# Banded attention in 48-query blocks, values stationary, pipelined by batch with the MLP

A kernel that ran attention over all keys and then an MLP is replaced by one that computes only a band, and runs the MLP of one batch inside the attention of the next. The question is what that does to the time, and what sets the time of the new kernel.

## The chip, the cores and the metric

One core of one Trainium2 chip. Times are device microseconds (us) of one execution. A core has engines that run side by side: PE (TensorE matmuls; PEld is its weight load), DVE (VectorE), ACT (ScalarE), POOL (GpSimd), SP (SyncE, which here only starts transfers). PE writes its results into tiles in PSUM (`psA` and the `ps_` pools below); another engine reads a tile there, and until it has, PE waits with the next result for that tile.

## The reference, cut to what matters

Shapes: 8 batches, 8 heads, 576 positions, head size 64; then 4608 tokens of width 512, and a hidden width of 2048. The result is float32.

```python
scores = scale * np.matmul(q, k.transpose(0, 1, 3, 2))
mask = np.abs(pos[:, None] - pos[None, :]) <= 32
mask = mask | is_global[:, None] | is_global[None, :]     # 8 global positions
scores = np.where(mask, scores, -1000000000.0)
attn = softmax(scores)                                    # cut: max, exp, sum
x = (attn @ v), heads side by side, 4608 x 512
h = x @ w_in
s = np.sin(alpha * h)
g = h + s * s / (alpha + 1e-09)
return g @ w_out
```

A query outside the global set therefore needs 65 keys around it and the 8 global keys. Only the 8 global queries need all 576 keys.

## The kernel before: what the change touches

It works on one pair of heads after the other. For each head it computes all 576 x 576 scores, multiplies the exponentials by a 0/1 mask, and multiplies with the values, where the exponentials are the stationary operand. The values carry a column of ones, so that the softmax sum comes out beside them. Only when all 8 batches are done does the MLP start. All weights are scaled on DVE, and they are first used at 470 us. (`...` marks cuts.)

```python
for b in range(B):
    ...
    for hp in range(NHP):                       # 4 pairs of heads
        ...                                     # transposes of q and k
        for t in range(2):
            for g in range(NKG):
                for gi in range(GK):            # 6 key tiles of 96 in all
                    nc.tensor.matmul(out=scm[:, gi, :], lhsT=kTh[:, k0 : k0 + KW], rhs=qTh[:, 0:SM], ...)
                    nc.tensor.matmul(out=sct[:, gi, :], lhsT=kTh[:, k0 : k0 + KW], rhs=qTh[:, SM:S], ...)
                nc.scalar.activation(out=E[...], in_=scm[:, :, :], func=AF.Exp, scale=scale)
                nc.scalar.activation(out=E[...], in_=sct[:, :, :], func=AF.Exp, scale=scale)
                nc.vector.tensor_tensor(out=E[...], in0=E[...], in1=MASK[...], op=ALU.mult)
            for qb in range(NQB):
                for kt in range(NKT):
                    nc.tensor.matmul(out=avq[0:qrows, qb, :], lhsT=E[:, kt, qs0 : qs0 + qrows],
                                     rhs=VS[:, hh * NKT + kt, :], ...)
            ...                                 # reciprocal and normalization on DVE, transposes to xT
for tci in range(NCHUNK):                       # the MLP, 9 chunks of 512 tokens
    for nt in range(NT):
        for c in range(CT):
            nc.tensor.matmul(out=h2[:, :tn], lhsT=w_inp[:, c, nt * P : (nt + 1) * P],
                             rhs=xT[:, c, t0 : t0 + tn], ...)
        nc.scalar.activation(out=Sb[:, :tn], in_=h2[:, :tn], func=AF.Sin)
        nc.vector.tensor_tensor(out=S2[:, :tn], in0=Sb[:, :tn], in1=Sb[:, :tn], op=ALU.mult)
        nc.vector.tensor_tensor(out=H2b[:, nt, :tn], in0=h2[:, :tn], in1=S2[:, :tn], op=ALU.add)
    ...                                         # second matmul, copy, store
```

The softmax here doesn't subtract the row's maximum and nothing guards it: scores larger than these inputs give would overflow.

## Time and profile before

| kernel before | value |
|---|---|
| median of 3 runs | 733.84 us (732.45 to 734.54) |
| profiled span | 732.5 us |
| PE busy | 642.0 us, 88% |
| DVE, ACT, POOL busy | 56%, 47%, 15% |
| granted PE clock | 1.00 throughout |

The head of the page gives the busy time of each engine and its share of the span; the PE row cuts the span into 40 slices, a digit being the busy share in tenths.

```profile
PE 642.0 (88%) x4360; PEld 352.6 (48%) x4384; DVE 412.0 (56%) x893; ACT 341.7 (47%) x566; POOL 107.7 (15%) x144
...
PE   0000699999999999999999999999999999999997
```

The PE row has a quiet start of four slices, one slice at six tenths, and is at nine tenths or more from there almost to the end. Where PE is full, PE is what to save. The windows view says it in numbers; the columns are the stretch, its length, then busy time (with the number of instructions) of PE, PEld, DVE, ACT and POOL, the granted clock, the DMA share and GB/s.

```profile
0.00:79.00 79.00, 0.64 (x6) 0.61 (x7) 37.67 (x62) 0.00 (x0) 40.31 (x60) 1.00 1.51 165
250.00:350.00 100.00, 100.00 (x842) 62.14 (x841) 58.44 (x143) 58.92 (x99) 22.47 (x28) 1.00 0.90 37
```

PE is busy in 100.00 of 100.00 us in the middle of the attention. In the first 79 us it does nothing worth naming. The waits view gives for each wait the engine and its line, the engine that released it, then the total, the number of times and the longest.

```profile
PE psx L237 <- POOL identb masks.py:199: 43.0, 1, 43.0
PE psx L237 <- DVE qT L242: 36.0, 2, 35.5
```

The chain of waits (the page's fourth part) is the work that ended last, followed back. It is PE's:

```profile
PE 83%; issue 6%; DVE 3%; POOL 3%; DMA 2%; ACT 2%; DVEq 0%; ACTq 0%; POOLq 0%
```

In the groups (line, engine, operation, output<-inputs, shape, count, then total busy us and mean ns, then idle time before it) the score and value matmuls are the attention's largest cost:

```profile
L259 PE MATMUL scm<-qT,kT 64*96 64x512 bf16 x384 | 202.2, 646 | 2.0 <-ACT E L273 0.9
L297 PE MATMUL avq<-VS,E 96*128 96x65 bf16 (+1 forms) x1920 | 143.3, 245 | 1.1 <-DVE E L285 0.8
```

### The profile page before, as it was taken

The page shows a single profiled execution, that of the slowest core. Times are in us where ns is not written, and L with a number is a line of the kernel's source. Part 1 is how long each engine was busy: PE and PEld are TensorE (multiplying, and loading weights), DVE is VectorE, ACT ScalarE, POOL GpSimd, SP SyncE. Part 2 cuts the span into 40 slices and gives each one's busy share as a digit, 9 for nine tenths or more (in the row PEclk, how much of TensorE's full clock was granted, in tenths as well). Part 3 has the DMA queues.
Part 4 walks back from the last instruction along what each step waited for, and adds up shares of the span by engine and source line. Part 5 has one row for each costly group of instructions (what it writes and reads, how often), then busy time and mean ns, then how long its engine had stood idle before and what let it go on. Part 6 is the DMA issues. An engine that isn't in the chain of part 4 may idle for free.

```text
span 732.5 us, 10762 instructions
## 1 busy us (share of the span) xinstructions
PE 642.0 (88%) x4360; PEld 352.6 (48%) x4384; DVE 412.0 (56%) x893; ACT 341.7 (47%) x566; POOL 107.7 (15%) x144
## 2 busy tenths in 40 slices
PE   0000699999999999999999999999999999999997
PEld 0000356555665656565656666544444444444443
DVE  2466355555565655555555565594483573673762
ACT  0000465655565655555555565553353353353442
POOL 5167040122140131221500000000000000000000
PEclk9999999999999999999999999999999999999999
DMA  9999264918993999559968000001101001001001
GB/s 244 294 46 122 5 41 27 34 12 55 33 61 21 23 62 33 33 34 34 66 19 15 1 1 1 1 1 57 44 16 58 30 29 57 30 30 57 29 31 57
DMA packets 122529, 33.74 MB, mean 46 GB/s; under 512 B 115184, under 2 KB 115184, under 8 KB 121840
## 3 DMA queue, kind: packets, MB, share of 16 engines
q0 software_dynamic: 112256, 14.16, 49.3%
q1 hardware_dynamic: 10224, 18.89, 7.2%
q8 instruction: 34, 0.56, 0.3%
q14 instruction: 15, 0.12, 0.1%
HBM read 37.77 MB, written 9.44 MB: 64 GB/s over the span
## 4 chain that ended last, share of the span: by engine, by line
PE 83%; issue 6%; DVE 3%; POOL 3%; DMA 2%; ACT 2%; DVEq 0%; ACTq 0%; POOLq 0%
PE scm L259 21%; PE avq L297 17%; PE ops L383 17%; PE psx L237 5%; PE sct L266 5%; PE xps L329 2%; DMA QS<-in_q_dram 2%; DVE H2b L374 1%; ACT E L273 1%; POOL VS L79 1%; ACT Sb L369 1%; PE xps L335 1%; DVE Cq L111 1%; POOL KS L72 0%; POOL QS L72 0%
## 5 line engine op out<-in xcount | busy, mean ns | idle before, releaser
L273 ACT ACTIVATE E<-scm 96x1024 bf16<-96x1024 f32 x192 | 195.8, 1020 | 41.1 <-PE scm L259 35.8
L259 PE MATMUL scm<-qT,kT 64*96 64x512 bf16 x384 | 202.2, 646 | 2.0 <-ACT E L273 0.9
L285 DVE TENSOR_TENSOR E<-E,MASK 96x1152 bf16<-96x1152 bf16 x192 | 143.2, 747 | 24.9 <-ACT E L279 24.7
L297 PE MATMUL avq<-VS,E 96*128 96x65 bf16 (+1 forms) x1920 | 143.3, 245 | 1.1 <-DVE E L285 0.8
L297 PEld LDWEIGHTS <-E 96*128 96x128 bf16 (+1 forms) x1920 | 116.5, 135 | 53.1 <-issue 16.1
L383 PE MATMUL ops<-w_outp,H2b 128*128 128x512 bf16 x565 | 139.1, 379 | 0.6
L279 ACT ACTIVATE E<-sct 96x128 bf16<-96x128 f32 x192 | 51.8, 270 | 114.8 <-PE sct L266 114.4
L361 PEld LDWEIGHTS <-w_inp 128*128 128x128 bf16 x576 | 56.1, 98 | 74.3 <-issue 10.5
L383 PEld LDWEIGHTS <-H2b 128*128 128x128 bf16 x576 | 55.5, 98 | 68.8 <-DVE H2b L374 5.1
L266 PEld LDWEIGHTS <-kT 64*96 64x96 bf16 x384 | 58.4, 181 | 35.7 <-issue 26.7
L266 PE MATMUL sct<-qT,kT 64*96 64x64 bf16 x384 | 66.8, 264 | 0.0
L259 PEld LDWEIGHTS <-kT 64*96 64x96 bf16 x384 | 58.1, 173 | 15.3 <-issue 3.0
L391 ACT COPY osb<-ops 128x512 f32<-128x512 f32 x36 | 21.1, 585 | 84.3 <-PE ops L383 84.3
L237 PE MATMUL psx<-identb,QS 96*128 96x96 bf16 x192 | 21.9, 277 | 43.0 <-POOL identb masks.py:199 43.0
L237 PE MATMUL psx<-identb,KS 96*128 96x96 bf16 x192 | 26.2, 276 | 36.0 <-DVE qT L242 36.0
L305 DVE RECIPROCAL rec<-avq 128x4 f32<-128x4 f32 x64 | 11.7, 183 | 78.6 <-PE avq L297 78.6
L72 POOL DMA_DIRECT2D QS<-in_q_dram x48 | 36.9, 777 | 79.3 <-PE psx L237 78.5
L237 PEld LDWEIGHTS <-QS 96*128 96x128 bf16 x192 | 14.7, 133 | 57.2 <-issue 48.7
L237 PEld LDWEIGHTS <-KS 96*128 96x128 bf16 x192 | 15.4, 130 | 50.6 <-issue 50.6
L72 POOL DMA_DIRECT2D KS<-in_k_dram x48 | 36.9, 775 | 17.2 <-PE psx L237 15.1
L273 ACT ACT_TABLE_LOAD x1 | 1.3, 1283 | 81.5 <-PE sct L266 81.5
L242 DVE COPY kT<-psx 128x576 bf16<-128x576 bf16 x32 | 14.6, 455 | 33.0 <-PE psx L237 33.0
(614 smaller groups left out, 592.7 us busy)
## 6 DMA issues: line engine op xcount, KB each, us to landing
out_dram<-osb SPq DMA_DIRECT2D x36, 256.0 KB, 2.0
QS<-in_q_dram POOLq DMA_DIRECT2D x48, 96.0 KB, 3.6
KS<-in_k_dram POOLq DMA_DIRECT2D x48, 96.0 KB, 3.8
VS<-in_v_dram POOLq DMA_DIRECT2D x8, 576.0 KB, 11.1
wtmp<-in_moe_w_in_dram SPq DMA_DIRECT2D x4, 1024.0 KB, 8.4
alphaB<-in_moe_alpha_dram SPq DMA_DIRECT2D x1, 1024.0 KB, 5.8
wtmp_4073<-in_moe_w_out_dram SPq DMA_DIRECT2D x1, 1024.0 KB, 12.2
wtmp_4079<-in_moe_w_out_dram SPq DMA_DIRECT2D x1, 1024.0 KB, 10.4
```

The source lines that it names most:

```text
L72: nc.gpsimd.dma_start(out=dstS[:, jt, :, :], in_=src[b, :, jt * KW : (jt + 1) * KW, :].rearrange("h p d -> p h d"),)
L237: nc.tensor.transpose(out=psx[:, jt * KW : (jt + 1) * KW], in_=srcS[:, jt, 2 * hp : 2 * hp + 2, :], identity=identb[0:KW, 0:KW],)
L259: nc.tensor.matmul(out=scm[:, gi, :], lhsT=kTh[:, k0 : k0 + KW], rhs=qTh[:, 0:SM], start=True, stop=True,)
L266: nc.tensor.matmul(out=sct[:, gi, :], lhsT=kTh[:, k0 : k0 + KW], rhs=qTh[:, SM:S], start=True, stop=True,)
L273: nc.scalar.activation(out=E[:, g * GK : (g + 1) * GK, 0:SM], in_=scm[:, :, :], func=AF.Exp, scale=scale,)
L279: nc.scalar.activation(out=E[:, g * GK : (g + 1) * GK, SM:S], in_=sct[:, :, :], func=AF.Exp, scale=scale,)
L285: nc.vector.tensor_tensor(out=E[:, g * GK : (g + 1) * GK, :], in0=E[:, g * GK : (g + 1) * GK, :], in1=MASK[0:KW, g * GK : (g + 1) * GK, :] ...
L297: nc.tensor.matmul(out=avq[0:qrows, qb, :], lhsT=E[:, kt, qs0 : qs0 + qrows], rhs=VS[:, hh * NKT + kt, :], start=(kt == 0), stop=(kt == NK ...
L329: nc.tensor.transpose(out=xps[:, qs0 : qs0 + QB], in_=xnp[:, qb, :], identity=identb[:, :],)
L361: nc.tensor.matmul(out=h2[:, :tn], lhsT=w_inp[:, c, nt * P : (nt + 1) * P], rhs=xT[:, c, t0 : t0 + tn], start=(c == 0), stop=(c == CT - 1),)
L383: nc.tensor.matmul(out=ops[:tsn, :], lhsT=H2b[:, nt, ts0 : ts0 + tsn], rhs=w_outp[:, nt, :], start=(nt == 0), stop=(nt == NT - 1),)
L391: nc.scalar.copy(out=osb[:tsn, :], in_=ops[:tsn, :])
```

## The change

It was meant to do less work and to fill what is left. Scores and values are computed for blocks of 48 queries against their 112 neighbouring keys and the 8 global keys. Two heads go into one matmul: the key block of both is stationary, and the queries are laid out block-diagonally. The values become the stationary operand, and so the result already comes out transposed as the MLP wants it. A matmul with ones gives the softmax sum (`den`); its reciprocal is exp(-ln(den)) on ACT. Global queries gather their sums from all blocks (`gn`, `gd`). Then the loop over batches is pipelined: the second MLP matmul of batch p-1 is cut into pieces that fill PE between the steps of the attention of batch p. The order on every engine is as written; no scheduler moves anything.

The diff cut to its core (the old attention loop above goes out whole; `...` marks cuts):

```diff
+    psA = ctx.enter_context(tc.tile_pool(name="psA", bufs=1, space=bass.MemoryType.PSUM))
 ...
+    def stage_T(b, hp):                                   # transposes
+        ...                                               # 6 into Kps, copied to kTw by DVE
+        Qps = psA.tile([P, S], BF, name="h2")
+        for jt in range(NTW):
+            nc.tensor.transpose(out=Qps[...], in_=QS[...], identity=identb[0:TW, 0:TW])
+        for t in range(2):
+            nc.vector.tensor_copy(out=qBD[hp][pr, :, :, t, 0:QB]..., in_=Qps[pr, :]...)
+    def stage_Q(b, hp, par):                              # scores
+        Sp = psA.tile([P, 2, CH], F32, name="Sp")
+        for u in range(NU):                               # 6 matmuls of 112 columns
+            nc.tensor.matmul(out=Sp[...], lhsT=kTw[hp][:, par, u, :], rhs=qBD[hp][:, par, u, :, :], ...)
+        E = epool.tile([P, 2, EW], BF, name="E")
+        nc.scalar.activation(out=E[:], in_=Sp[:, :, 0:EW], func=AF.Exp, scale=scale)
+        nc.vector.tensor_tensor(out=Ev, in0=Ev, in1=MASK[...], op=ALU.mult)
+    def stage_V(b, hp, par, E, xTb, gn, gd):              # values
+        num = psA.tile([P, 2, CH], F32, name="num")
+        den = psA.tile([P, NU, QC], F32, name="den")
+        ...                                               # 2 matmuls with ones into den, 6 into num
+        nc.scalar.activation(out=lnd[:], in_=den[:], func=AF.Ln)
+        nc.scalar.activation(out=rec[:], in_=lnd[:], func=AF.Exp, scale=-1.0)
+        for t in range(2):
+            nc.vector.tensor_tensor(out=xv[...], in0=numv[pr, :, :, t, 0:QB], in1=rec[pr, ...], op=ALU.mult)
+        for t in range(2):
+            nc.vector.tensor_reduce(out=gn[pr, par, hp, :], in_=numv[pr, :, :, t, QB:QC]..., op=ALU.add)
+        nc.vector.tensor_reduce(out=gd[:, par, hp, :], in_=den[:, :, QB:QC]..., op=ALU.add)
+    def stage_G(b, xTb, gn, gd):                          # global rows
+        ...                                               # 4 small DVE operations
+        for j in range(NG):
+            nc.gpsimd.tensor_copy(out=xTb[:, :, bass.ds(pregs[j], 1)], in_=xg[:, :, j : j + 1])
+        nc.vector.tensor_copy(out=xT[:, :, b * S : (b + 1) * S], in_=xTb[:])
 ...
+    def weight_slots():                                   # run between the steps of batch 0
+        for c in range(CT):
+            eng = nc.vector if c < 2 else nc.gpsimd
+            eng.tensor_tensor(out=w_inp[:, c, :], in0=wtmp[:], in1=alphaB[:], op=ALU.mult)
+        ...
+            nc.gpsimd.tensor_scalar(out=w_outp[:, t, :], in0=wtmp2[:, ti, :],
+                                    scalar1=recipT[:, t : t + 1], scalar2=None, op0=ALU.mult)
 ...
+    CYC = (("h2", 1), ("num", 2), ("den", 1), ("Sp", 2))  # PSUM tiles of the first MLP matmul
+    def mm1(c, H2b):
+        ...                                               # 4 matmuls of 512 columns per 128 hidden units
+        nc.scalar.activation(out=Sb[:, 0:n, :], in_=h2[:], func=AF.Sin)
+        nc.gpsimd.tensor_tensor(out=S2[:, 0, :], in0=Sb[:, 0, :], in1=Sb[:, 0, :], op=ALU.mult)
+        if n == 2:
+            nc.vector.tensor_tensor(out=S2[:, 1, :], in0=Sb[:, 1, :], in1=Sb[:, 1, :], op=ALU.mult)
+        ...                                               # DVE adds h + S2 one step later
 ...
+    TAIL = 4
+    for p in range(NCH):
+        if 1 <= p < B:
+            fill = mm2(p - 1, H2[p - 1], ("ops", "ops", "h2", "ops"))     # 16 pieces
+            parts, last = attention(p)                    # units: V(j) after Q(j+2)
+            nf = len(fill) - TAIL
+            merge(parts, fill[:nf], nf / len(parts))
+            last()
+            for f in fill[nf:]:
+                f()
+        ...
+        m1 = mm1(p, H2[p])
+        if p + 1 < B:
+            m1.insert(7, nxt)                             # global columns and stage_T(p + 1, 0)
+            m1.insert(9, partial(stage_T, p + 1, 1))
+        merge(m1, fill, 1.5)
```

A batch thus has two stages: the attention stage, from its first score matmul, with 8 units (4 pairs of heads, 2 parities of blocks) and most of the second matmul of the batch before; and the stage of the first MLP matmul. Every PSUM tile exists once.

## The prediction

> **What bounds it now.** The windows view has three phases. Start: PE does almost nothing for the first 79 us. It waits for staged loads, for the identity that GpSimd makes late, and for masks (waits view: "PE psx <- POOL identb" 43.0 us, "PE psx <- DVE qT" 36.0). Attention, to about 470 us: PE busy 100.00 of 100 us between 250 and 350; the chain of waits repeats every 12.1 us, one pair of heads, x32 = 387 us. MLP: 1,152 matmuls of 512 columns about 0.22 us apart, PE busy 98%. PE bounds everything after the start; DVE is 56% busy, ACT 47%.
>
> **What the change does, from durations in the trace.**
> - Scores and values are computed only in 48-query blocks of 112+8 keys. PE per pair of heads: 24 small matmuls of 112 columns, 4 of 336, 12 transposes. avq pairs (load plus 65 columns) run 64 ns apart, transposes about 77 ns: an estimate of 24x0.065+4x0.145+12x0.077 = 3.1 us instead of 12.1. Over 32 pairs 387 becomes about 98 us. Stationary operands become 128 wide: the Trainium skill's "TensorE: Matmul & The Clock Gate", weight-path perf modes, gives the fast load only to those; the trace agrees (64x96 loads 173-181 ns, 128x128 98 ns).
> - ACT: exponentials shrink from 192x(1.02+0.27) us to 64x0.75, plus 64 Ln and 64 Exp of about 0.47 us. DVE: mask 64x0.50 instead of 192x0.75, but 128 normalizations of about 0.45 us, 192 reduces of about 0.2 and wider copies: near 25 us a batch.
> - The MLP work is unchanged (249 us of PE at 216 ns); half of it (the second matmul) fills PE beside the next batch's attention. PE floor: 98+249 = about 347 us.
>
> **Why the floor is not reached.** Every PSUM tile is single.
> - Attention: values of unit j+1 wait until DVE freed num/den of unit j: den matmuls 0.5, Ln 0.45, Exp 0.48, two normalizations 0.9, three reduces 0.65, about 3.1 us a unit. Eight units, a lead-in with a table load (1.28), two late transposes and the global rows at the end (eight dependent GpSimd copies, then xT) give about 32 us, more than PE's 24.
> - First matmul: 11 squares go to GpSimd. The skill's "GPSIMD Engine Reference", section 3.1, gives 4,497 ns for a two-input op of 2,048 fp32; I estimate 1.2 us for 512 (no trace shows one yet). With 12 small copies in between GpSimd needs about 17 us against PE's 15.7 with transposes: about 18.5 us.
> - Period about 50.5 us, seven times 353. Before that: loads, gathers, masks and unfilled attention of batch 0, with GpSimd also scaling weights, about 79 us, then 18.5. After it: 28.5 (both matmuls merged) + 14.3 + 2.
>
> 79+18.5+353+28.5+14.3+2 = **about 495 us, range 440 to 545**. Faster by over 2%: 0.98; within: 0.01; slower: 0.01.
>
> **What would show it.** PE busy about 350-390 us, about 75% of the span. Attention-unit period near 3.1 us, ended by DVE reduces releasing num/den (waits: PE num/den <- DVE). GpSimd squares near 1.2 us, and PE waiting in the first matmul for DVE adds which wait for GpSimd. First MLP matmul near 79 us. ACT and DVE each under 75%.
>
> **What would make it wrong.** GpSimd squares much slower or DVE slowed beside them (mm1 over 22 us); overlap between stages better than I assume (toward 440); loads of 128-byte packets unable to keep one batch per 50 us; longer start-up waits for weights.

## The result, and the profile after

Ratios here are the mean time of one kernel's runs over that of the kernel before in the same rounds, so not quite the ratio of the medians quoted. Executions over 1.5% slower than the fastest of the same kernel are left out of the means.

| | before | after |
|---|---|---|
| median us (same rounds) | 733.14 | 575.41 (574.28 to 575.82) |
| ratio, 95% interval | | 0.7848 (0.7835 to 0.7862) |
| profiled span | 732.5 | 572.6 |
| PE busy | 642.0 | 362.7 |
| DVE busy | 412.0 | 331.5 |
| ACT busy | 341.7 | 220.4 |
| POOL busy | 107.7 | 307.9 |

The new kernel takes 21.5% less time. But 575.4 us lies outside the predicted range of 440 to 545. The page after:

```profile
PE 362.7 (63%) x2396; PEld 186.8 (33%) x2440; DVE 331.5 (58%) x702; ACT 220.4 (38%) x343; POOL 307.9 (54%) x451
...
PE   0124220776586768666866587767676767678996
...
PEclk9999999979999999899989988999999989999999
...
issue 28%; POOL 24%; PE 20%; DVE 8%; ACT 7%; DMA 6%; ACTq 3%; SPq 1%; POOLq 0%; DVEq 0%
```

PE lost 279 us of busy time, as intended, and is now nowhere full except at the end. No engine is over 63%, and the chain of waits is spread over all of them: the time is now made of waits between engines. The PE clock, 1.00 before, dips in some slices.

The following table cuts the span at the first matmul of each MLP stage (read from the timeline view) and sets it beside the sum in the prediction.

| stretch | predicted us | measured us | difference |
|---|---|---|---|
| start, to the first MLP matmul | 79 | 102.3 | +23.3 |
| seven attention stages, mean of one | 32 | 35.8 | +3.8 x 7 |
| seven stages of the first MLP matmul, mean of one | 18.5 | 22.3 | +3.8 x 7 |
| the two together, seven periods | 353 | 407.1 | +54.1 |
| end, from the eighth such stage | 63.3 | 63.1 | -0.2 |
| sum | 495.3 | 572.6 | +77.3 |

(The measured column is rounded line by line.) So the sum was short in three pieces. Each has its lines in the trace.

**The start.** The first line below is the first MLP matmul in PE's timeline (start, duration, engine, line, operation; the bracket is the idle time before it, with its releaser); then POOL's timeline from 65 us on:

```profile
102.32 0.58 PE L540 MATMUL h_854<-xT,w_inp 128*128 128x512 bf16 x1 [22.76 <-DVE xT L416]
...
65.38 7.00 POOL L482 TENSOR_SCALAR w_outp<-wtmp,recipT 128x512 bf16<-128x512 f32 x4
...
89.46 6.19 POOL L482 TENSOR_SCALAR w_outp<-wtmp,recipT 128x512 bf16<-128x512 f32 x4
...
99.41 2.06 POOL L413 COPY xTb<-xg 128x4 bf16 x8
```

and from the groups by form:

```profile
L482 POOL TENSOR_SCALAR w_outp<-wtmp,recipT 128x512 bf16<-128x512 f32 x16 | 25.6, 1609 | 0.1
L466 DVE TENSOR_TENSOR w_inp<-wtmp,alphaB 128x2048 bf16<-128x2048 f32 x2 | 10.6, 5316 | 0.1
```

POOL works without a gap from 52.81 to 99.41 us: 9.5 us of `w_inp` products, 25.6 us of `w_outp` scalings, and 11.5 us (the rest of the 46.6) for issues of loads for batch 1. Only then come the eight global copies of batch 0, which stand behind all of it in POOL's order. The first MLP matmul needs them through `xT`. The last values of batch 0 had begun at 78.3 us, over 20 us before. (The two products of DVE took 5.79 and 4.85 us because POOL's stood beside them; e12 shows it.)

**The attention stage.** The windows view of one attention stage (242 to 277) and of the stage before it (219 to 242), in the columns given above:

```profile
219.00:242.00 23.00, 17.87 (x94) 8.32 (x97) 12.81 (x20) 9.27 (x12) 13.02 (x22) 0.93 0.18 44
242.00:277.00 35.00, 22.72 (x190) 12.54 (x191) 23.43 (x63) 16.83 (x30) 18.24 (x29) 1.00 0.91 78
```

PE is busy 22.72 of 35 us in the attention stage, at full clock. What it waits for (`PE den`, in all of the run):

```profile
PE den L363 <- DVE gd L398: 82.4, 56, 7.7
```

and DVE's timeline in one unit:

```profile
199.87 0.51 DVE L351 TENSOR_TENSOR E<-E,MASK 128x672 bf16<-128x672 bf16 x1
201.39 0.92 DVE L385 TENSOR_TENSOR xTb<-num,rec 64x288 bf16<-64x288 f32 x2 [1.01 <-ACT rec L380]
202.34 0.42 DVE L393 TENSOR_REDUCE gn<-num 64x8 f32<-64x48 f32 x2
202.78 0.21 DVE L398 TENSOR_REDUCE gd<-den 128x8 f32<-128x48 f32 x1
```

The `den` matmuls of a unit wait for `gd`, the last of DVE's five operations on the unit before; then DVE waits 1.01 us for `rec`, because Ln and Exp could not start before the new `den`. Each waits for the other, as in a ring. The units are 3.15 us apart without transposes and 3.27 us on average, about what was predicted (3.1). (Where a unit also copies transposed keys and queries, as the one before this does, DVE has no idle time: its `gd` comes 3.76 us after the last one.) A whole stage is 35.8 us: 6.0 from its first scores to its first values (the start of its first `den` matmul), 22.9 from the first to the last values, 6.9 for the tail (last unit, global rows and the four last pieces of fill).

**The stage of the first MLP matmul.** PE's timeline in its second half; `xN` is the number of instructions in a row, and the bracket is the idle time before with its releaser.

```profile
230.15 0.42 PE L323 MATMUL h_2096<-identb,QS 96*128 96x96 bf16 x6 [1.10 <-DVE H2b L525]
...
236.24 1.85 PE L540 MATMUL h_2136<-xT,w_inp 128*128 128x512 bf16 x4 [2.50 <-DVE qBD_88 L330]
237.88 2.81 PE L540 MATMUL num<-xT,w_inp 128*128 128x512 bf16 x8
240.53 1.03 PE L540 MATMUL den<-xT,w_inp 128*128 128x512 bf16 x4
```

and the same place one batch earlier:

```profile
180.12 1.04 PE L540 MATMUL h_1568<-xT,w_inp 128*128 128x512 bf16 x4 [2.50 <-DVE qBD_88 L330]
```

The query transposes of the next batch use the PSUM tile `h2`, which is also one of the tiles of the MLP's cycle. PE waits 1.10 us until `h2` is free for the transposes, and 2.50 us until DVE has copied the transposed queries out of it (`qBD`), though DVE does that late, in order, behind adds. In the stage at 219 us, eight matmuls after this take 2.81 us that take 1.89 at full clock; one batch earlier the same wait stands, and no matmul after it is slower (four in 1.04 us instead of 1.85). Seven such stages lasted 25.2, 20.3, 22.0, 22.0, 24.7, 20.3 and 21.9 us, at granted clocks of 0.86, 1.00, 0.92, 0.92, 0.79, 1.00 and 0.92: the same code, with the same two waits in each, varies with the clock it got. Two stages had no drop of the clock and took 20.3 us. The drops came as stretches at 0.50 of about 3.4 us (236.3 to 239.7) or twice that (120.3 to 127.1). POOL is busy only 13.02 of the 23 us.

### The profile page after: what moved, and what is told of

The parts are those of the page before. It is cut to its first block, busy times and chain, and to the rows that moved or that the text cites. A ratio compares the mean times of both kernels' runs of the same rounds, so it can differ in the third digit from the quotient of the medians.

```text
span 572.6 us, 7365 instructions
## 1 busy us (share of the span) xinstructions
PE 362.7 (63%) x2396; PEld 186.8 (33%) x2440; DVE 331.5 (58%) x702; ACT 220.4 (38%) x343; POOL 307.9 (54%) x451
## 4 chain that ended last, share of the span: by engine, by line
issue 28%; POOL 24%; PE 20%; DVE 8%; ACT 7%; DMA 6%; ACTq 3%; SPq 1%; POOLq 0%; DVEq 0%
PE num L540 7%; ACT Sb L547 5%; POOL w_outp L482 4%; PE ops L576 4%; POOL QS L103 3%; POOL KS L103 3%; DVE H2b L525 3%; PE Sp L540 3%; DMA QS<-in_q_dram 2%; POOL VW_92 L110 2%; POOL xTb L413 2%; ACTq L175 2%; DMA wtmp<-in_moe_w_in_dram 2%; POOL w_inp L466 2%; ACT L547 1%
## 5 line engine op out<-in xcount | busy, mean ns | idle before, releaser
L576 PE MATMUL ops<-w_outp,H2b 128*128 128x512 bf16 x412 | 103.1, 379 | 1.7 <-ACT osb L583 0.7
L385 DVE TENSOR_TENSOR xTb<-num,rec 64x288 bf16<-64x288 f32 x128 | 58.2, 455 | 58.4 <-ACT rec L380 57.3
L363 PE MATMUL den<-E,ones_77 128*128 128x336 bf16 x64 | 21.3, 333 | 89.8 <-DVE gd L398 82.4
L378 ACT ACTIVATE lnd<-den 128x336 f32<-128x336 f32 x64 | 28.9, 452 | 111.8 <-PE den L363 100.9
L349 ACT ACTIVATE E<-Sp 128x672 bf16<-128x672 f32 x64 | 46.6, 729 | 48.0 <-PE Sp L342 47.7
L540 PE MATMUL num<-xT,w_inp 128*128 128x512 bf16 x204 | 58.7, 426 | 4.2 <-DVE H2b L525 3.3
L547 ACT ACTIVATE Sb<-num 128x1024 bf16<-128x1024 f32 x27 | 27.7, 1024 | 37.1 <-PE num L540 34.9
L363 PEld LDWEIGHTS <-ones_77 128*128 128x128 bf16 x64 | 6.2, 97 | 104.2 <-DVE gd L398 103.4
L351 DVE TENSOR_TENSOR E<-E,MASK 128x672 bf16<-128x672 bf16 x64 | 32.6, 512 | 9.3 <-ACT E L349 8.1
L540 PE MATMUL Sp<-xT,w_inp 128*128 128x512 bf16 x140 | 33.6, 379 | 0.2
L380 ACT ACTIVATE rec<-lnd 128x336 f32<-128x336 f32 x64 | 31.0, 484 | 2.0
L540 PE MATMUL den<-xT,w_inp 128*128 128x512 bf16 x108 | 28.4, 387 | 0.0
L547 ACT ACT_TABLE_LOAD x8 | 10.3, 1283 | 41.6 <-PE h_854 L540 24.3
```

Of the source, the lines that this page charges most:

```text
L349: nc.scalar.activation(out=E[:], in_=Sp[:, :, 0:EW], func=AF.Exp, scale=scale)
L351: nc.vector.tensor_tensor(out=Ev, in0=Ev, in1=MASK[:, par, :, None, :].to_broadcast([P, NU, 2, QC]), op=ALU.mult,)
L363: nc.tensor.matmul(out=den[:].rearrange("p u c -> p (u c)"), lhsT=on[:], rhs=E[:].rearrange("p a (u t c) -> p (a u) t c", t=2, c=QC)[:, :, ...
L378: nc.scalar.activation(out=lnd[:], in_=den[:], func=AF.Ln)
L380: nc.scalar.activation(out=rec[:], in_=lnd[:], func=AF.Exp, scale=-1.0)
L385: nc.vector.tensor_tensor(out=xv[:, :, :, par, :], in0=numv[pr, :, :, t, 0:QB], in1=rec[pr, :, 0:QB].rearrange("p (a u) c -> p a u c", a=2 ...
```

## The experiments

Fourteen kernels ran, all timed in three or more rounds beside the kernel before (732.7 to 733.0 us median). All gave right results but e15. The quoted expectations may shorten theories to letters, which stand for the following (where a quoted text spells a theory out, its own words hold). R: the attention unit is a ring through the reduce that stands last on DVE; rivals D (DVE's own throughput) and P (PE with its fill) hold it. B: the PSUM bank shared between queries and MLP holds the first MLP stage; rival G: POOL's work does. S: the weight scalings on POOL, and POOL's order, set the start; rival W: the arrival of the weights does, whoever scales them. M and Q (e6), L (e10), C (e12) and X (e14) are spelled out with their runs. The experiments follow by question, not by date.

| run | edit | median us | ratio |
|---|---|---|---|
| after | | 575.41 | 0.7848 |
| e1 | reduces before normalizations | 529.95 | 0.7225 |
| e2 | queries in another bank | 551.11 | 0.7519 |
| e3 | `w_outp` scaled on ACT | 561.88 | 0.7662 |
| e4 | no fill in the attention | 655.14 | 0.8940 |
| e6 | weight loads earlier | 571.71 | 0.7804 |
| e8 | global columns copied earlier | 577.26 | 0.7882 |
| e15 | no table switches (wrong result) | 563.62 | 0.7682 |
| e5 | e1 + e2 + e3 | 485.19 | 0.6625 |
| e9 | e5 + e6, values before next scores | 488.42 | 0.6645 |
| e10 | e5, Sin table and second transposes moved | 498.62 | 0.6809 |
| e11 | e5, six tail pieces | 490.74 | 0.6695 |
| e12 | e5, all `w_inp` products on DVE | 491.54 | 0.6703 |
| e13 | e5 + e6 + e10 + e11 + e12 | 507.84 | 0.6916 |
| e14 | e5, Sin table moved only | 483.44 | 0.6601 |

### e1: what holds an attention unit

The same DVE operations in another order: the three reduces first. `gd` reads `den` and needs no `rec`.

```diff
         numv = ...
+        nc.vector.tensor_reduce(out=gd[:, par, hp, :], in_=den[:, :, QB:QC]..., op=ALU.add)
+        for t in range(2):
+            nc.vector.tensor_reduce(out=gn[pr, par, hp, :], in_=numv[pr, :, :, t, QB:QC]..., op=ALU.add)
         for t in range(2):
             nc.vector.tensor_tensor(out=xv[...], in0=numv[...], in1=rec[...], op=ALU.mult)
-        for t in range(2):
-            nc.vector.tensor_reduce(out=gn[...], ...)
-        nc.vector.tensor_reduce(out=gd[...], ...)
```

> The three reduces of an attention unit are issued before the two normalizations instead of after them; DVE's work is the same. Theory R (the cycle of the single num/den tiles holds a unit at 3.15 us: denominators, Ln, Exp, normalizations, reduces, next denominators): the reduces (0.2 + 0.2 + 0.2 us) move into the time in which DVE waits for Ln and Exp, so a unit falls to about 2.6 us and the whole by 8 x 8 x 0.55 = 35 us, to about 540. Theory D (DVE's throughput holds the attention stage): nothing changes, 575. Theory P (PE holds it): nothing changes.

Measured: 529.95 us, 45.5 us less. The first to the last values of a batch went from 22.9 to 16.9 us, a unit from 3.27 to 2.42 us, and the attention stage from 35.8 to 29.4. The MLP stage (22.1 us on average) and the start (104.2 us) changed little. DVE in two units:

```profile
195.77 0.21 DVE L382 TENSOR_REDUCE gd<-den 128x8 f32<-128x48 f32 x1
195.90 0.41 DVE L389 TENSOR_REDUCE gn<-num 64x8 f32<-64x48 f32 x2
196.32 0.92 DVE L397 TENSOR_TENSOR xTb<-num,rec 64x288 bf16<-64x288 f32 x2
197.28 0.51 DVE L351 TENSOR_TENSOR E<-E,MASK 128x672 bf16<-128x672 bf16 x1
197.89 0.21 DVE L382 TENSOR_REDUCE gd<-den 128x8 f32<-128x48 f32 x1
```

and the wait that was 82.4 us:

```profile
PE den L363 <- DVE gd L382: 14.0, 10, 8.7
```

In this stretch DVE passes from one unit to the next without idle time, 2.1 us for a unit without copies (195.77 to 197.89). The ring is open: with `den` free early, the next unit's `den` matmuls, Ln and Exp run beside this unit's normalizations. DVE's work and PE's are the same as before the edit, so neither D nor P can have held the unit in the kernel after. The gain was larger than expected, since Ln and Exp left the path as well. What comes next seems to be DVE's own throughput, D one step later; that is read from this timeline, and no run took work off DVE to test it.

### e2: which bank the queries pass through

```diff
-    def stage_T(b, hp):
+    def stage_T(b, hp, qtag="h2"):
-        Qps = psA.tile([P, S], BF, name="h2")
+        Qps = psA.tile([P, S], BF, name=qtag)
 ...
-                stage_T(p + 1, 0)
+                stage_T(p + 1, 0, "ops")
-            m1.insert(9, partial(stage_T, p + 1, 1))
+            m1.insert(9, partial(stage_T, p + 1, 1, "ops"))
```

> The two query transposes issued inside the first MLP matmul write the bank of ops, idle then, instead of the bank of h2. Theory B (the 3.6 us in which PE stands there, 1.1 waiting for the H2b add that frees h2 and 2.5 waiting for the query copies in h2, and the half clock that follows the wait, make this stage 20.3 to 25.2 us instead of the 18.5 predicted): the stage falls to about 18 us with a granted clock of 1.00, the whole by 20 to 35 us, to 540 to 555. Theory G (GpSimd's squares and copies set the stage): the wait moves to other lines, the stage stays above 20 us and the whole above 567.

Measured: 551.11 us, 24.3 us less. The MLP stage took 18.1 to 19.7 us (20.5 the first time). The two waits of 1.10 and 2.50 us are gone, and one on the key copy has grown, from 0.18 us to 1.44:

```profile
282.51 0.41 PE L308 MATMUL Kps<-identb,KS 96*128 96x96 bf16 x6 [1.44 <-DVE kTw L314]
...
284.48 1.89 PE L540 MATMUL num<-xT,w_inp 128*128 128x512 bf16 x7
```

The matmuls after it run at full clock here (1.89 us for seven in a row; the trace drops a record now and then). But four of the seven stages still had a granted clock of 0.91; the three others were at 1.00. So the shared bank was the cause of the larger part. Comparing stages at a clock of 1.00 only, they fell from 20.3 to 18.1 us: 2.2 us for the waits alone, of 3.15 us on average. The rest is fewer and shorter drops of the clock.

### e8: does POOL's work hold the MLP stage?

The twelve small POOL copies (`globals_in`) move from the MLP stage into the attention stage before it.

```diff
+                if j == n - 2 and b + 1 < B:
+                    for hp in range(NHP):
+                        globals_in(b + 1, hp)
 ...
-                for hp in range(NHP):
-                    globals_in(p + 1, hp)
```

> The 12 GpSimd copies of global keys and queries, 3.5 us in the middle of the first MLP matmul, go into the attention stage, where GpSimd stands idle for 15.6 us. Theory G (GpSimd sets the first-matmul stage, as the prediction had it): the stage loses about 3 us, the whole about 20 us, to 555. Theory B (the shared query bank and DVE's order set it): within 4 us of 575.

Measured: 577.26 us. The MLP stage stayed at 20.3 to 24.2 us, and the start got 4.4 us longer (106.7): batch 1's copies now stand on POOL before the global copies of batch 0, which again shows what ends the start. POOL's copies do not hold the MLP stage; rival G, that POOL's busy time sets it, is refuted, and with it the prediction's reason for the length of this stage. The squares themselves stayed on POOL: in the stage at 219 us DVE waits 0.33 us for one of them three times, which no run removed.

### e3 and e6: what makes the start long

In e3 the sixteen scalings of `w_outp` go from POOL to ACT.

```diff
-                    nc.gpsimd.tensor_scalar(
-                        out=w_outp[:, t, :], in0=wtmp2[:, ti, :],
-                        scalar1=recipT[:, t : t + 1], scalar2=None, op0=ALU.mult,
+                    nc.scalar.activation(
+                        out=w_outp[:, t, :], in_=wtmp2[:, ti, :],
+                        func=AF.Copy, scale=recipT[:, t : t + 1],
                     )
```

> The 16 scalings of w_out go from GpSimd (1.6 us each) to ACT. Theory S (GpSimd's written order makes the start 23 us longer than predicted: the scalings cost 25.6 us instead of 11, and the global rows of batch 0 queue behind them): the first MLP matmul moves from 102 to about 86 us, the whole by about 15 us, to 560. Theory W (the start waits for the weights to arrive, whoever scales them): the first MLP matmul stays within 5 us of 102.

Measured: 561.88 us, 13.5 us less; the first MLP matmul at 90.46 us instead of 102.3. One scaling takes 708 ns on ACT, and POOL now waits for DVE:

```profile
87.59 2.03 POOL L413 COPY xTb<-xg 128x4 bf16 x8 [7.07 <-DVE xg L411]
```

About half of the miss at the start came back. POOL's train no longer ends the start; the attention of batch 0 does, and its last values began at 83.3 us instead of 78.3 (1.9 us of this already at its first values), with the scalings now in ACT's order. So 11.9 us is what the move gave net of that. In e6 the masks' scratch tiles are laid into the space of `w_outp`, so that the weight tiles get memory of their own and their loads need not wait for the mask:

```diff
+    early = w_outp[:].rearrange("p t n -> p (t n)")
-    MB = setup.tile([P, NU, 2, QC], F32, name="MB")
+    MB = early[:, 0:1344].bitcast(F32).rearrange("p (u a c) -> p u a c", u=NU, a=2)
 ...                                   (gN, gB, IQi and DQ likewise)
-    setup.release()
 ...
     wst.release()
+    setup.release()
```

> Only the memory changes: the setup tiles lie in w_outp's space instead of the space that the weight staging reuses, so the weight loads no longer wait 9.2 us for the mask. Theory M (the reuse makes the weights arrive late, and GpSimd's train of scalings and loads starts when they do): loads start at about 28 instead of 37.7 us, GpSimd's train starts near 44 instead of 52.8, the first MLP matmul is at about 94 instead of 102, the whole at about 567. Theory Q (the weights only share the queues with the loads of q, k and v, and arrive no sooner): under 2 us of change.

Measured: 571.71 us, 3.7 us less; first MLP matmul at 99.84. The loads were issued 7.6 us earlier (30.07 instead of 37.69), and POOL's train began 3.5 us earlier (49.27 instead of 52.81) but had the same work. The expectation of about 8 us was not met. With POOL's train in place, the weights' arrival is a small part.

### e4: does the fill cost or help?

All sixteen pieces of the second matmul go after the attention.

```diff
-    TAIL = 4
+    TAIL = 16
```

> The second MLP matmul of the batch before is no longer mixed into attention: all 16 of its pieces come after the last unit, beside the global rows. Theory R (units bound by the num/den cycle, PE has slack): the distance of the value matmuls stays near 3.15 us, and 12 pieces of 0.87 us are added per period less the 1.9 us in which PE now waits for xT: +8.5 us x 7 = about +60, to 635. Theory P (PE-bound attention): units shorten to about 2.3 us and the whole grows by less than 20 us.

Measured: 655.14 us, 79.7 us more, against 60 expected. The attention stage took 48.1 us, 17.7 of them the tail. The unit did not get shorter without PE's fill, as rival P has it; it got longer, 3.56 us. (The clock changed too, so it is e1 that rules P out cleanly.) The page's row of the granted clock, in tenths, for e4:

```profile
PEclk9999999855996589757985698569865997589999
```

PE's timeline, first of e4, then of the kernel after, the same six matmuls:

```profile
275.04 0.77 PE L371 MATMUL num<-E,VW 128*128 128x112 bf16 x6
```

```profile
247.70 0.46 PE L371 MATMUL num<-E,VW_92 128*128 128x112 bf16 x6
```

They took 0.77 us instead of 0.46. The granted clock was 0.55 to 0.58 from the first scores to the tail of the attention stages and 1.00 in four of the seven MLP stages between them, though in none of these attention stages was an idle time of PE longer than 2.53 us. The fill seems to pay twice: it does work in PE's gaps, and with it the clock of these stages was 1.00. That the missing 20 us are all clock is argued from these durations, not isolated.

### e15: what the table switches cost

ACT switches its function table twice a batch, for Ln and Exp and for Sin. Here the MLP uses Square in place of Sin, which needs no other table. The result is wrong (relative error 0.03).

```diff
-                    nc.scalar.preload_act_table_set("natural_log_exp_and_others")
+                    if b == 0:
+                        nc.scalar.preload_act_table_set("natural_log_exp_and_others")
 ...
-                nc.scalar.activation(out=Sb[:, 0:n, :], in_=h2[:], func=AF.Sin)
+                nc.scalar.activation(out=Sb[:, 0:n, :], in_=h2[:], func=AF.Square)
```

> The changed kernel with Square instead of Sin (wrong result on purpose) and no table load but the first: no switch of ACT's tables is left, all else is the same. If the two loads of 1.28 us per period lie on its chain, the lead-in falls from 6.0 to about 4.7 us and the first-matmul stage by about 1 us: 15 us or more of 575. If they are hidden, under 4 us.

Measured: 563.62 us, 11.8 us less, with one table load instead of sixteen. The time from first scores to first values fell from 6.0 to 4.6 us; five of the seven MLP stages changed by 0.3 us or less; the two longest fell by 1.1 and 1.3 us, at a granted clock 0.06 to 0.07 higher. The load that counts is the one at the head of the attention stage, in the kernel after (ACT's timeline):

```profile
242.31 1.28 ACT L435 ACT_TABLE_LOAD   x1
243.60 0.73 ACT L349 ACTIVATE E<-Sp 128x672 bf16<-128x672 f32 x1
```

It takes 1.28 us, and the exponential follows 0.01 us later.

### e5: the three edits together

> The edits of the first three runs together: reduces first, query transposes in the idle bank, w_out scaled on ACT. They saved 45.5, 24.3 and 13.5 us alone. If they act on three different stages (attention units, first MLP matmul, start), the savings add: 83 us, 492. If they share a limit (PE's clock or DVE), the sum falls short by over 10 us.

Edits of e1, e2 and e3. Measured: 485.19 us. The gains add to 45.5 + 24.3 + 13.5 = 83.3 us; together they gave 90.2. First MLP matmul at 85.13 us (17.2 less than after), attention stages 28.9 to 29.4 us, MLP stages 18.1 to 19.3 us, end 62.8 us. The page:

```profile
PE 355.8 (74%) x2440; PEld 182.6 (38%) x2440; DVE 329.3 (68%) x702; ACT 229.5 (48%) x359; POOL 282.8 (59%) x435
...
PE   0132422978987889788888888888888888898996
...
PEclk9999999999999999999989999999899999999999
```

The work is that of the kernel after; PE's share rose from 63% to 74%, and the clock is nearly whole. The start shrank 5.3 us beyond e3's: the first values of batch 0 came 1.5 us sooner, and from the first to the last took 3.9 us less. That this one program comes near the predicted 495 us is chance: 45.5 us of its gain are e1's, from a ring that the prediction had right; e2 and e3 together gave 37.8 of the 80 us missed.

### e9 to e14: attempts to go below e5

**e9** puts V(j) before Q(j+2), and adds e6.

```diff
-            parts += [first, second]
+            parts += [first, second] if j < 0 else [second, first]
```

> All edits so far that helped (reduces first, query bank, w_out on ACT, weights early) and one more: in a step of attention the value matmuls of unit j come before the scores of unit j+2. The lead-in of 6.0 us before the first values loses about 1.5 us, as they no longer wait behind scores, transposes and a fill piece; seven or eight times 1.5 = about 11 us, plus about 8 us for early weights: about 473 us. If the units are now bound by PE (about 2.4 us of PE work a unit), they stay at 2.4 us.

Measured: 488.42 us is the median of all four runs, of which one was slow; the three fast ones are 484.1, 486.9 and 490.0 us, not to be told apart from e5. First scores to first values fell by 1.9 us (from 5.5 to 3.7 in most stages), but first to last values rose from 16.9 to 18.2. The stage gained next to nothing. The first MLP matmul came at 84.67 us instead of 85.13, so e6's earlier loads and the swap together are worth next to nothing at the start once `w_outp` is off POOL.

**e10** loads the Sin table ahead, right after the last attention unit, and moves the second transposes two slots on. **e14** does the first of these alone.

```diff
     last()
+    nc.scalar.preload_act_table_set("trig_and_small")
 ...
-            m1.insert(9, partial(stage_T, p + 1, 1, "ops"))
+            m1.insert(11, partial(stage_T, p + 1, 1, "ops"))     # e10 only
```

> On top of e5: the table load for Sin (1.28 us) is issued right after the last attention unit, where ACT stands idle, and the second pair of transposes of the first MLP matmul comes two pieces later. Theory L (in this stage the loss left over is latency at its start and the 1.4 us in which PE waits for the key copy, followed by half clock): the stage falls from 18.1 to 19.3 us to about 17 us at a granted clock of 1.00, the whole by 8 x 1.5 = 12 us, to 473. Rival: PE-bound already, under 4 us.

> On top of e5: only the early table load for Sin; the transposes stay where e5 has them. The run before it (e10) changed both and came out 13 us slower than e5, with the stage of the first MLP matmul 1 us shorter and the lead-in of attention 2.5 us longer. Theory X (the later transposes do the harm: their query copy holds the ops bank that the first piece of the second matmul needs): this run is at or below e5's 485, by up to 8 us. Rival: the early load does the harm, near 498.

Measured: e10 498.62 us, e14 483.44 us. In e10 the MLP stage was the shortest of all (17.7 us after the first), but first scores to first values took 7.9 to 9.0 us. PE at the head of the attention stage in e10:

```profile
157.80 1.89 PE L577 MATMUL ops<-w_outp,H2b 128*128 128x512 bf16 x4 [2.27 <-DVE qBD L330]
159.48 0.77 PE L342 MATMUL Sp<-qBD,kTw 128*128 128x112 bf16 x6
```

The first piece of fill waits 2.27 us for the bank `ops`, where the late queries still lie, and goes on at half clock: four matmuls in 1.89 us, against 1.03. The wait was moved from one stage into the next, where it costs more. e14 shows that the table had no part in it (theory X, that the later transposes did the harm, is right). e14 against e5 is 0.6601 (0.6574 to 0.6627) against 0.6625 (0.6609 to 0.6640): not to be told apart.

**e11** keeps six pieces for the tail (`TAIL = 6` in e5).

> On top of e5: 6 instead of 4 pieces of the second MLP matmul are kept for the time in which the global rows are made. If PE still stands 1.86 us per period waiting for xT, the two pieces (1.7 us) fill it and the attention units get 1.7 us less PE work: the whole falls by 7 x 1.7 = 12 us, to 473, if units are PE-bound now; if the num/den cycle still holds the units at 2.42 us, the pieces taken out of them gain nothing but the wait is filled for nothing: within 3 us of 485.

Measured: 490.74 us, 5.5 more than e5. First scores to first values fell to 4.7 us, first to last values rose to 19.0. With fewer pieces the rounding puts two of them between one pair of value steps and none between the next; whether that is the cause was not isolated.

**e12** does all `w_inp` products on DVE in e5. Theory C: DVE's products are slow because POOL's run beside them.

```diff
-                eng = nc.vector if c < 2 else nc.gpsimd
+                eng = nc.vector
```

> On top of e5: all four w_in scalings on DVE. Theory C (DVE's 128x2048 product takes 2.29 us in the kernel before and alone, but 4.9 to 5.8 us while GpSimd runs its own product of two SBUF tensors): each takes 2.3 us, the four 9.2 us against 7.3 to 10.6 for two; GpSimd has no product left and the first MLP matmul comes 3 to 8 us sooner than e5's 85. Rival (slow because of DMA traffic into the same memory): they stay at 4 to 5 us each and the start grows by 8 us or more.

Measured: 491.54 us, with the groups line

```profile
L466 DVE TENSOR_TENSOR w_inp<-wtmp,alphaB 128x2048 bf16<-128x2048 f32 x4 | 9.2, 2291 | 0.1
```

C holds: a product that took 5.32 us on average in the kernel after takes 2.29 us with no product of POOL beside it. The traces show that the later of the two waits: in the kernel after, POOL's first product ran from 52.81 to 57.31 us, and DVE's, begun at 53.67, ended at 59.46, about one product's length later. It holds for more than products. In e5, while POOL's second product runs from 61.13 to 66.08 us, a mask of DVE takes 4.80 us instead of 0.51:

```profile
61.65 4.80 DVE L351 TENSOR_TENSOR E<-E,MASK 128x672 bf16<-128x672 bf16 x1
```

The time of e12 still got worse, with the first MLP matmul at 90.3 us instead of 85.1, but not by the products: the first values of batch 0 were 5.5 us late (49.87 us instead of 44.38) before the first product ran (58.41). DVE's first masks stand behind the reciprocal of `recipT`, and its load came later. DVE's timeline of e12, then of e5:

```profile
49.20 0.25 DVE L458 RECIPROCAL recipT<-recipT 128x16 f32<-128x16 f32 x1 [10.73 <-DMA recipT<-in_moe_alpha_dram]
```

```profile
43.71 0.25 DVE L458 RECIPROCAL recipT<-recipT 128x16 f32<-128x16 f32 x1 [6.15 <-DMA recipT<-in_moe_alpha_dram]
```

From the first values to the first MLP matmul both take about the same (40.4 and 40.7 us). In e12 POOL, with no product to do, issued fourteen loads of batch 1 between 32.8 and 44.2 us; in e5 it issued four, and the next at 59.5. That these crowded out the load of `recipT` fits the times, but was not tested.

**e13** joins e5, e6, e10, e11 and e12.

> All edits together: e5, Sin table early with later transposes, 6 tail pieces, w_in on DVE, weights' own memory. If each gives what its own run is expected to give, about 485 - 12 - 6 - 5 - 8 = 455 us; if the units or the start share one limit, 465 to 475.

Measured: 507.84 us. The start is the shortest (83.8 us) and the MLP stage is 17.7 us, but the attention stage took 33.1 to 34.0 us at a granted clock of about 0.90. The lead-in was long again (6.9 to 8.3 us) as in e10, and the units too (18.6 to 20.7 us from first to last) as in e11.

The fastest version found is e5, or e14, which is not separable from it: 0.66 of the time before, and by the medians (483 to 485 against 575 us) 0.84 of the time after.

## Why the prediction was right or wrong

It said faster by over 2%, with 0.98, and that was right. It said 495 us with 440 to 545, and 575.41 us was measured: wrong in size by 80 us, with the range too narrow. The mechanism was partly right.

**Right.**
- That PE bounds the kernel before, and that its work falls to 350 to 390 us: 362.7 measured. Because the span was longer than predicted, this is 63% of it and not 75%.
- That the attention unit is a ring through single PSUM tiles, ended by DVE's reduces, of about 3.1 us: 3.15 measured, and 82.4 us of waiting of `den` for `gd`. e1 showed the ring.
- POOL's squares at 1.2 us: 1.04 to 1.28. ACT at 38% and DVE at 58% are under 75%. Weight loads of 128x128 take 97 to 104 ns, as the trace before had them. The stretch from the eighth MLP stage on, 63.3: 63.1 measured, in part by luck: its first stage, without transposes, took 16.4 us instead of 18.5, and what follows the last matmul 4.3 instead of 2.

**Wrong: "with GpSimd also scaling weights, about 79 us".** The start took 102.3 us. The text gave no duration for a scaling; behind it was an estimate of 0.7 us each, 11 us in all. They took 1.61 us each, 25.6 us in all. And the step that failed behind the size is one of order: the global copies of batch 0 stand on POOL after all weights and all load issues, so that POOL's train, and not the attention, ends the start. e3 gave back 11.9 us of the 23.3, e5 17.2. For the last 6 us the trace of e5 names two candidates that no run isolates: DVE's first masks wait 6.15 us for the load of `recipT`, and later a DVE product and a mask wait behind POOL's products (4.97 us instead of 2.29, 4.80 instead of 0.51).

**Wrong: "GpSimd needs about 17 us against PE's 15.7 with transposes: about 18.5 us".** The stage took 22.3 us on average. The duration of a square was right, but POOL was busy for 13 of 23 us and moving work off it changed nothing (e8). PE's idle time before the `num` matmuls of this stage that ended with an add of DVE (`H2b`) was 3.3 us in the whole run. What held PE was a bank: the queries' transposes pass through `h2`, a tile of the MLP's cycle, and DVE empties it late. That was the overlooked wait, 1.10 + 2.50 us in each of the seven stages; in five of them half clock came on top. e2 removed both waits and left a mean of 19.2 us, near the predicted length for another reason. The prediction had listed "mm1 over 22 us" among what would make it wrong, but for POOL's sake.

**Wrong in size: "Eight units, a lead-in with a table load (1.28), two late transposes and the global rows at the end ... about 32 us".** The stage took 35.8 us. The units were right (22.9 us for seven distances). Eight units of 3.1 leave 7.2 us of the 32 for all else, which the text does not divide. Measured at 3.15 a unit, the rest is 10.6 us: 6.0 for the lead-in, from first scores to first values, 0.8 for the late transposes and 3.8 for the global rows. The lead-in, for which the text names only the load of 1.28 us, is the term most likely mis-sized. The table load is 1.4 us of it (e15). Another 1.9 us go when the first values no longer stand behind the third scores, transposes and fill (e9, on top of e5), though e9's units gave this back. In the stage at 241 us PE also waits 1.67 us for the first exponential before it may write the second scores; that was not tested.

**Not thought of: the clock.** It was 1.00 before, with PE busy 100 of 100 us. In the kernel after, with gaps, it is part of the time: single MLP stages went to 0.79, and e4's attention to 0.58.

**Open.** What the same MLP stage gets as clock, with the same waits in it, varies from batch to batch (20.3 to 25.2 us), and no run says what decides it. Why the 2 us that e9 gained in the lead-in came back in the units was not found, nor why e11 lost.

## What to carry to other kernels

When one bottleneck engine is relieved, list for each PSUM tile and each in-order engine who frees it and in which place of the order: putting the operation that frees a tile first (e1) and taking the query transposes out of a shared bank (e2) gave 45.5 and 24.3 us without removing any work. Cost every operation that moves to another engine by a duration measured there, and look at what stands behind it in that engine's order; e3's sixteen scalings were a quarter of the start. Ask too what a relieved engine will start sooner: with POOL free, e12's loads came earlier and a small one that DVE needed came later. Gaps of PE cost more than their length when the clock drops, and a wait that is moved into another stage (e10) is not removed.

## What the Trainium skill lacked or had wrong

- The Trainium skill's "GPSIMD Engine Reference", section 4.1, Engine selection, calls one-input operations on GpSimd "roughly line-rate". Here a one-input scaling of 128x512 from float32 to bf16 took 1,609 ns on POOL (mean; 1,550 in the quickest group of four), against 708 ns on ACT (e3) and 469 to 797 ns (means of groups of four) for the same operation on DVE in the kernel before. Someone who goes by the page sizes this wrong by a factor of 2 or more.
- The same page, section 1, Specifications, says that GpSimd shares its SBUF interfaces with VectorE and contends with it when an operation has two SBUF inputs. That agrees: a 128x2048 product on DVE took 2.29 us alone (e12) and 4.85 to 5.79 us beside POOL's (after), and a mask of 0.51 us took 4.80 (e5). Its figure of 4,497 ns for a POOL operation of 2,048 elements, section 3.1, agrees (4,498 ns the shortest in after), and the prediction's use of it for 512 did as well.
- The Trainium skill's "TensorE: Matmul & The Clock Gate", section "Why this matters for your kernels", asks for no idle gap over about 3 us. In e4 the granted clock was 0.55 to 0.58 in the attention stages up to their tails, with no gap over 2.53 us in any, and in the kernel after half clock followed gaps of 1.10 and 2.50 us in five of seven stages. Its section "A second HAM failure mode: psum-queue depth-cycling" has frequent short gaps do the same; that agrees, but it does not tell how much idle in short gaps is too much. The same code with the same gaps got 0.79 to 1.00 here.
- The Trainium skill's "ScalarE: Activation LUTs", section "What ACT_TABLE_LOAD costs", gives 1,283 ns and about 1,380 ns of drain for each switch. The load agrees (1,283 ns), the drain was not seen: the load started 0.02 us after the ACTIVATE before it ended, the next ACTIVATE 0.01 us after the load, and taking the switch away saved 1.4 us a batch (e15).
